# An attention-and-mixer kernel: in batches 4 and 6, v loads issued after the transposes of u, two features moved from VectorE to ScalarE, and k.v two slots later

## The chip, the cores and the metric

The kernel runs on one core of one Trainium2 chip. The metric is the time of one execution in microseconds (us) of device time. The kernel before was timed three times: 294.59, 293.90 and 294.26 us, median 294.26 us. The core has a matrix engine (TensorE, PE in the profile, with its weight loads as PEld), VectorE (DVE), ScalarE (ACT), GpSimd (POOL) and SyncE (SP), which here only issues DMAs. Each engine works through its own queue in the order in which the program gave it instructions, and waits on semaphores for what other engines or DMAs must have finished first.

## The reference

The inputs are q, k and v with 8 batches, 8 heads, 576 positions and 64 features per head, and the weights U, V, w1 and w2 of a mixer. Cut to what matters:

```python
# attention, per batch and head; c, s are cosine and sine weights of the position
q_p = concat(relu(q) * c, relu(q) * s)        # 128 features
k_p = concat(relu(k) * c, relu(k) * s)
kv  = k_p^T @ v            # 128 x 64
z   = sum over positions of k_p
x   = (q_p @ kv) / (q_p @ z + 1e-6)           # heads side by side: 576 x 512
# mixer, per batch
u   = x + (x^T @ U @ V)^T  # low rank mixing over positions
out = u + relu(u @ w1) @ w2                   # 512 -> 2048 -> 512
```

## The kernel before

**Tiles.** The 576 positions of a batch are four chunks of 128 rows (c = 0 to 3) and a tail of 64 (c = 4). Products take bf16 inputs and add in f32 PSUM banks.

**One list of slots.** The matrix work of the mixer is cut into 272 units, called slots, in one list (`lay_all`, L1057). Per batch there are the first units (u times w1, then relu: `g1_main` L670 and `g1_part` L596), and then the second units (the hidden layer times w2: `w_part` L829, 14 units, or `g2_part` for batch 0); behind odd batches there are units for the tails of the pair. `starts[b]` is the slot in which the first units of batch b begin: 0, 32, 70, 100, 138, 168, 202 and 232 for b = 0 to 7. Batches 3 and 5 are in `MIXED`: their first units use products of sums of blocks with seven multiplications in place of eight, whose right-hand sides (`tb`, four VectorE subtractions of blocks of the transposed u, `uT_form` L584) are formed in the four slots ahead of `starts[b]`. Their units come in the order `HALF = ("1", "s4", "6 2", "s5", "5 7", "s6", "3", "s7 4")`, where a digit is a part of the seven (`g1_part`) and "s4" to "s7" are plain units (`g1_main`). After a part or a plain unit, ScalarE (parts 1, 6, 5, 3 and all plain units) or VectorE (parts 2, 7, 4) takes the result out of PSUM.

**Work laid beside the slots.** The attention of batch b runs beside the mixer of the two batches before it. `attention_plan(b)` (L1083) names a slot for every step; after each slot's matrix unit, the steps planned for it are given to their engines, in the order of the batches. So a step's slot is its place in the queues, not a time. For b = 3 to 7 the steps are:

- `feature`: relu and weight of one chunk and one of cos and sin, first for q, then for k, 20 operations from slot F on. F is `starts[b-2]` + 16 for the batches 4 and 6, where G, which is `starts[b-1]`, lies 14 slots behind F. In each slot ScalarE takes one operation, and in some slots VectorE takes the next one as well.
- `v_prep`: casts of v to bf16 by GpSimd, from slot V0 on, which is `starts[b-2]` + 9.
- `qtr_dma`: transposes of q's features, as DMAs from SyncE's queue: tail, chunks 0 and 1, chunks 2 and 3.
- `kv_pair` (L344): 40 matrix products, k.v for all heads; they need every feature of k and every chunk of v. ScalarE takes the result out of PSUM (b > 3).
- `x_unit` for the five chunks (x from q's transposed features and k.v, with VectorE for the division), then `A_unit`, `u_va` and `u_add` (the low-rank part of u), then `utr_dma` (L518): the transposes of u, as DMAs from SyncE's queue, for the halves d = 0, 1 and d = 2, 3 and, in odd batches, for the tail rows.
- the loads of q, k and v of batch b + 1 (`loads` L983), at the three slots `at_load`. Each is three DMA issues on SyncE's queue (the tail L93, the odd rows L80, the even rows L87). The tiles for q, k and v as loaded are single, so each load waits until the features or casts of batch b have read the tile.

The slots that matter below are these. For b = 4: F = 86, G = 100, V0 = 79; the loads of q, k and v of batch 5 are at slots 94, 100 and 84, and k.v is at slot 101. At slots 84 and 86 lie the transposes of the u of batch 3 (both halves, and the tail at 86). For b = 6: F = 154, G = 168, V0 = 147; the loads of batch 7 are at 162, 168 and 152, k.v at 169; the transposes of the u of batch 5 at 151 and 153. The first `x_unit` is at G + 5 = 105 and 173.

Of the kernel before, what the change touches and what calls it, by code (L numbers as in the profile page):

```python
# [17 lines left out]
def kernel(  # L18
# [100 lines left out]
    V_, A_, G_ = nc.vector, nc.scalar, nc.gpsimd  # L119
# [125 lines left out]
    G3, T1, X1, OA, OB, O1 = ("g", 3), ("T", 1), ("X", 1), ("oA", 1), ("oB", 1), ("O", 1)  # L245
    X1S = ("x", 1)
# [528 lines left out]
    MIXED = {3: (0, 2), 5: (0, 2)}  # L775
# [207 lines left out]
    def loads(b):  # L983
        def thunk(dst, src):
            def go():
                load_tail(dst, src, b)
                load_main(dst, src, b)

            return go

        return thunk(qst, q), thunk(kst, k), thunk(vst, v)
# [91 lines left out]
    def attention_plan(b):  # L1083
        plan = []
        odd = b % 2 == 1

        def put(at, f, *a):
            plan.append((at, lambda: f(b, *a)))

        ops = [(f, c, i) for f in (q_prep, k_prep) for c in QORD for i in range(2)]  # L1090
        if b == 2:
            for n, (f, c, i) in enumerate(ops):
                if n < 8:
                    put((25, 26, 27, 28, 28, 29, 29, 30)[n], feature, f, c, i, A_)
                elif n < 10:
                    put(24 + n, feature, f, c, i, V_)
                else:
                    put(
                        (34, 34, 35, 36, 37, 38, 39, 39, 40, 41)[n - 10], feature, f, c, i,
                        A_ if n in (14, 17) else V_,  # L1100
                    )
            V0 = 33
            at_q, at_load = (32, 34, 36), (37, 42, 43)
            kv_at, x_at, a_at, u_at = 43, (44, 46, 48, 50, 52), 54, 55
            a_bank = O1
        else:
            F, G = starts[b - 2] + (20 if odd and b < B - 1 else 16), starts[b - 1]
            for s_ in range(G - F):
                for eng in (A_, V_)[: 1 + (s_ in ((0, 1, 2, 10, 11, 12) if b > 3 else (1, 2, 10, 11, 12)))]:
                    if ops:  # L1110
                        put(F + s_, feature, *ops.pop(0), eng)
            V0 = starts[b - 2] + 9 if b > 3 else F + 9
            at_q, at_load = (F + 5, F + 7, F + 7), (F + 8, F + 14, V0 + 5)
            if b == 3:
                at_q = (F + 6, F + 7, F + 8)
                at_load = (F + 11, F + 14, V0 + 5)
            X0 = G - 2 if odd else G
            x_at = [
                X0 + i for i in ((2, 4, 6, 9, 11) if b == 3 else (2, 4, 6, 8, 10) if odd else (3, 5, 7, 9, 11))
            ]  # L1120
            kv_at = X0
            if b in (4, 6):
                kv_at, x_at = G + 1, [G + i for i in (5, 8, 13, 16, 18)]
            elif b - 1 in MIXED:
                kv_at, x_at = G + 1, [G + i for i in ODDX]
            a_at = x_at[4] + (3 if b in (4, 6) else 2)
            u_at = a_at + 1
            a_bank = T1 if b == 3 else OB
        for n, c in enumerate(QORD):
            put(V0 + n, v_prep, 0, H, (c,), (G_,))  # L1130
        for at_, (c0, c1) in zip(at_q, ((4, 5), (0, 2), (2, 4))):
            put(at_, qtr_dma, c0, c1)
        put(kv_at, kv_pair, *X1)
        for n, c in enumerate(ORD):
            put(x_at[n], x_unit, c, *((O1, X1)[n % 2] if b < 4 else X1))
        put(a_at, A_unit, *a_bank, A_)
        put(u_at, u_va, (0, *X1), (2, *O1) if b < 4 else (2, OA, OB))
        put(u_at, u_add, 0)
        put(u_at + 2, u_add, 2)
        put(u_at + 2, utr_dma, 0, 2)  # L1140
        put(u_at + 4, utr_dma, 2, 4)
        if odd:
            put(*((u_at + 1, u_tail, *T1) if b < 4 else (u_at + 3, u_tail, *X1S)))
            put(u_at + 4, utr_dma, 4, 5)
        if b < B - 1:
            for at_, t in zip(at_load, loads(b + 1)):
                plan.append((at_, t))
        return plan
# [238 lines left out]
    for b in range(2, B):  # L1387
        for at, t in attention_plan(b):
            put(at, t)
# [34 lines left out]
```

## Time and profile before

| what | value |
|---|---|
| median of three runs | 294.26 us (293.90 to 294.59) |
| profiled execution, its own time | 294.26 us |
| span of its trace | 292.4 us |
| PE busy | 284.8 us, 97% of the span |
| DVE busy | 226.5 us, 77% |
| ACT busy | 159.8 us, 55% |
| POOL busy | 67.7 us, 23% |
| granted clock of TensorE | 1.00 throughout |
| moved by DMA | 53.32 MB, mean 182 GB/s |

The span runs from the first to the last instruction of the trace; the execution's own time is 1.86 us longer. A line of a timeline gives start, duration, engine, source line, operation, tiles and count, and in square brackets the idle time of the engine ahead of it with what ended that time; "L521" is line 521 of the kernel. The line of a helper stands for all its callers: L80, L87 and L93 are the loads of q, k and v, told apart by the tile (`qst`, `kst`, `vst`); L521 and L527 are the transposes of u and of its tail; L301 and L299 are features on VectorE and ScalarE; L350 is k.v. A stretch's table gives the busy time of each engine in it and the number of instructions. Durations of matrix products include the depth of the array: where products follow each other, the distance from start to start is the cost.

### The profile page before, as it was taken

The page shows a single profiled execution, that of the slowest core. Times are in us where ns is not written, and L with a number is a line of the kernel's source. Part 1 is how long each engine was busy: PE and PEld are TensorE (multiplying, and loading weights), DVE is VectorE, ACT ScalarE, POOL GpSimd, SP SyncE. Part 2 cuts the span into 40 slices and gives each one's busy share as a digit, 9 for nine tenths or more (in the row PEclk, how much of TensorE's full clock was granted, in tenths as well). Part 3 has the DMA queues.
Part 4 walks back from the last instruction along what each step waited for, and adds up shares of the span by engine and source line. Part 5 has one row for each costly group of instructions (what it writes and reads, how often), then busy time and mean ns, then how long its engine had stood idle before and what let it go on. Part 6 is the DMA issues. An engine that isn't in the chain of part 4 may idle for free.

```text
span 292.4 us, 7406 instructions
## 1 busy us (share of the span) xinstructions
PE 284.8 (97%) x3040; PEld 206.1 (70%) x3066; DVE 226.5 (77%) x452; ACT 159.8 (55%) x278; POOL 67.7 (23%) x104
## 2 busy tenths in 40 slices
PE   8999999999999999989999999999999999999995
PEld 6876455545987546866887555886888548899884
DVE  4989738887898768948897367868899686769974
ACT  2955651576593466846594365946792552067100
POOL 8330600050052303640023400450021102200210
PEclk9999999999999999999999999999999999999999
DMA  6999999998939899699957994999084304020023
GB/s 205 354 260 254 266 188 254 295 237 217 275 102 150 225 364 188 160 250 184 294 153 152 238 300 95 252 220 319 10 141 87 147 3 89 38 108 1 2 85 132
DMA packets 85445, 53.32 MB, mean 182 GB/s; under 512 B 53988, under 2 KB 83076, under 8 KB 85412
## 3 DMA queue, kind: packets, MB, share of 16 engines
q1 hardware_dynamic: 78996, 41.62, 60.3%
q0 software_dynamic: 6272, 11.17, 15.8%
q8 instruction: 24, 0.39, 0.6%
q14 instruction: 9, 0.07, 0.1%
q10 hardware_dynamic: 144, 0.07, 0.1%
HBM read 36.86 MB, written 9.44 MB: 158 GB/s over the span
## 4 chain that ended last, share of the span: by engine, by line
PE 78%; DMA 12%; DVE 4%; SPq 2%; issue 2%; ACT 0%; POOL 0%; DVEq 0%; POOLq 0%
PE w_ps L848 23%; PE g_ps L680 19%; PE gt_ps L701 5%; PE o_ps L741 5%; PE al_ps L629 5%; DMA kst<-in_k_dram 5%; PE be_ps L629 4%; PE w_ps L202 3%; DMA vst<-in_v_dram 3%; PE x_ps L425 3%; DMA w_bf<-in_moe_w_ch_dram 3%; PE kv_ps L350 3%; PE ot_ps L761 2%; PE ot_ps L949 2%; DMA uT<-u_bf 2%
## 5 line engine op out<-in xcount | busy, mean ns | idle before, releaser
L680 PE MATMUL g_ps<-uT,w_bf 128*128 128x512 bf16 x366 | 90.7, 379 | 0.8
L689 ACT ACTIVATE hid<-g_ps 128x512 bf16<-128x512 f32 x96 | 57.0, 597 | 47.1 <-PE g_ps L680 39.0
L680 PEld LDWEIGHTS <-w_bf 128*128 128x128 bf16 x384 | 34.8, 98 | 34.2 <-DMA w_bf<-in_moe_w_ch_dram 0.2
L860 POOL TENSOR_TENSOR o_sb<-w_sum,u_bf 128x512 f32<-128x512 f32 x14 | 22.0, 1588 | 119.3 <-DVE w_sum L860 119.3
L848 PEld LDWEIGHTS <-hid 128*128 128x128 bf16 x448 | 43.6, 98 | 5.6
L848 PEld LDWEIGHTS <-S 128*128 128x128 bf16 x336 | 32.4, 98 | 4.8 <-issue 0.5
L848 PE MATMUL w_ps<-w_bf,hid 128*128 128x256 bf16 x224 | 26.9, 273 | 0.0
L848 PE MATMUL w_ps<-T,hid 128*128 128x256 bf16 x224 | 26.9, 273 | 0.0
L848 PE MATMUL w_ps<-T,S 128*128 128x256 bf16 x224 | 26.3, 273 | 0.0
L646 DVE TENSOR_TENSOR hid<-pw,be_ps 128x512 bf16<-128x512 f32 x24 | 16.4, 685 | 10.9 <-PE be_ps L629 5.8
L114 ACT ACTIVATE pw<-al_ps 128x512 f32<-128x512 f32 x24 | 14.2, 596 | 18.2 <-PE al_ps L629 17.4
L492 DVE TENSOR_TENSOR u_bf<-x_bf,va_ps 128x1024 bf16<-128x1024 bf16 (+1 forms) x20 | 19.5, 1001 | 3.9 <-PE va_ps L481 3.9
L860 DVE TENSOR_TENSOR o_sb<-o_sb,w_ps 128x512 f32<-128x512 f32 x28 | 19.1, 682 | 3.7 <-PE w_ps L848 3.1
L435 DVE TENSOR_TENSOR x_bf<-x_ps,rec 128x512 bf16<-128x512 f32 x28 | 19.4, 692 | 1.0
L715 POOL DMA_DIRECT2D out_dram<-o_sb x12 | 7.6, 631 | 44.7 <-DVE o_sb L860 22.2
L299 ACT ACTIVATE k_p<-kst,sinw 128x512 bf16<-128x512 f32 x26 | 17.1, 712 | 0.0
L701 PE MATMUL gt_ps<-uT_tl,w_bf 128*128 128x128 bf16 x256 | 16.4, 219 | 0.0
L116 POOL CAST v_ext<-vst 128x512 bf16<-128x512 f32 x24 | 15.7, 696 | 2.9 <-DMA vst<-in_v_dram 2.7
L741 PE MATMUL o_ps<-w_bf,hid 128*128 128x512 bf16 x61 | 15.3, 379 | 0.6 <-DMA w_bf<-in_moe_w_ch_dram 0.4
L816 DVE TENSOR_TENSOR S<-hid,S 128x1024 bf16<-128x1024 bf16 x14 | 15.3, 1096 | 0.1
L701 PEld LDWEIGHTS <-w_bf 128*128 128x128 bf16 x256 | 15.0, 98 | 0.4
L299 ACT ACTIVATE q_p<-qst,cosw 128x512 bf16<-128x512 f32 x21 | 14.4, 712 | 0.1
(187 smaller groups left out, 469.2 us busy)
## 6 DMA issues: line engine op xcount, KB each, us to landing
qst<-in_q_dram SPq DMA_DIRECT2D x14, 512.0 KB, 6.0
kst<-in_k_dram SPq DMA_DIRECT2D x14, 512.0 KB, 8.4
vst<-in_v_dram SPq DMA_DIRECT2D x12, 512.0 KB, 8.3
out_dram<-o_sb POOLq DMA_DIRECT2D x12, 512.0 KB, 5.8
w_bf<-in_moe_w_ch_dram POOLq DMA_DIRECT2D x8, 512.0 KB, 10.3
out_dram<-o_sb SPq DMA_DIRECT2D x4, 512.0 KB, 3.1
qst<-in_q_dram SPq DMA_DIRECT2D x2, 640.0 KB
kst<-in_k_dram SPq DMA_DIRECT2D x2, 640.0 KB, 10.9
```

The lines of the kernel that those rows point to most:

```text
L116: eng.tensor_copy(out=o, in_=i)
L299: nc.scalar.activation(out=o, in_=i, func=AF.Relu, bias=0.0, scale=w)
L435: nc.vector.tensor_tensor(out=x_of(b, c, rows).rearrange("p (g i d) -> p g i d", g=2, d=D), in0=view[:, :, :, 0:D], in1=rec[rows].unsqueez ...
L492: nc.vector.tensor_tensor(out=u_bf[b][:, d0 : d0 + n], in0=x_bf[b].rearrange("p c (d n) -> p d c n", n=P)[:, d0 : d0 + n], in1=t.rearrange ...
L629: nc.tensor.matmul(out=res[:, k_, :], lhsT=lhs[:, d, k_, :], rhs=rhs[:, d, :], start=(opens and k_ == 0 and d == 0), stop=(k_ == 1 and d = ...
L646: V_.tensor_tensor(out=o, in0=x, in1=res, op=ALU.add)
L680: nc.tensor.matmul(out=g_ps.rearrange("p (c t) -> p c t", c=4), lhsT=w1_bf[:, d, j * P : j * P + P], rhs=uT[b][:, d, :, :], start=(d == 0) ...
L689: nc.scalar.activation(out=hid[b][:, j, :], in_=g_ps, func=AF.Relu, bias=0.0, scale=1.0)
L701: nc.tensor.matmul(out=g_ps[:, jj, :], lhsT=w1_bf[:, d, j * P : j * P + P], rhs=uT_tl[pr][:, d, :], start=(d == 0), stop=(d == 3),)
L741: nc.tensor.matmul(out=o, lhsT=hid[0][:, j, cc * P : cc * P + P], rhs=w2_bf[:, j, :], start=(j == 0), stop=(j == NJ - 1),)
L848: nc.tensor.matmul(out=res[:, g, :], lhsT=lhs[:, k_, g * P : g * P + P], rhs=rhs[:, k_, :], start=(opens and k_ == 0 and g == 0), stop=(k_ ...
L860: eng.tensor_tensor(out=o, in0=x, in1=y, op=ALU.add)
```

## The change

It touches `attention_plan` alone. For the batches 4 and 6:

- VectorE takes the second operation in the slots F, F+1, F+2 and F+8, in place of F, F+1, F+2, F+10, F+11 and F+12. The list of 20 features then reaches two slots further, to F+15, which is G+1; all features of q stay where they were.
- k.v moves from G+1 to G+3.
- The load of the next batch's k moves from F+14 to F+16, and that of the next batch's v from V0+5 to V0+8.

The lines with `d0` stand for all batches.

```diff
         else:
             F, G = starts[b - 2] + (20 if odd and b < B - 1 else 16), starts[b - 1]
-            for s_ in range(G - F):
-                for eng in (A_, V_)[: 1 + (s_ in ((0, 1, 2, 10, 11, 12) if b > 3 else (1, 2, 10, 11, 12)))]:
+            late = b in (4, 6)
+            both = (0, 1, 2, 8) if late else (0, 1, 2, 10, 11, 12) if b > 3 else (1, 2, 10, 11, 12)
+            for s_ in range(G - F + 2 * late):
+                for eng in (A_, V_)[: 1 + (s_ in both)]:
                     if ops:
                         put(F + s_, feature, *ops.pop(0), eng)
             V0 = starts[b - 2] + 9 if b > 3 else F + 9
-            at_q, at_load = (F + 5, F + 7, F + 7), (F + 8, F + 14, V0 + 5)
+            at_q, at_load = (F + 5, F + 7, F + 7), (F + 8, F + (16 if late else 14), V0 + (8 if late else 5))
...
-            if b in (4, 6):
-                kv_at, x_at = G + 1, [G + i for i in (5, 8, 13, 16, 18)]
+            if late:
+                kv_at, x_at = G + 3, [G + i for i in (5, 8, 13, 16, 18)]
...
-        put(u_at, u_add, 0)
-        put(u_at + 2, u_add, 2)
-        put(u_at + 2, utr_dma, 0, 2)
-        put(u_at + 4, utr_dma, 2, 4)
+        d0 = 2 if odd and b - 1 in MIXED else 0
+        put(u_at, u_add, d0)
+        put(u_at + 2, u_add, 2 - d0)
+        put(u_at + 2, utr_dma, d0, d0 + 2)
+        put(u_at + 4, utr_dma, 2 - d0, 4 - d0)
         if odd:
-            put(*((u_at + 1, u_tail, *T1) if b < 4 else (u_at + 3, u_tail, *X1S)))
-            put(u_at + 4, utr_dma, 4, 5)
+            put(*((u_at + 1, u_tail, *T1) if b < 4 else (u_at + 3 + d0, u_tail, *X1S)))
+            put(u_at + 4 + d0, utr_dma, 4, 5)
```

## The prediction

> **What bounds the kernel now.** I read the page first: its busy times and its chain of work that ended last.
>
> ```profile
> PE 284.8 (97%) x3040; PEld 206.1 (70%) x3066; DVE 226.5 (77%) x452; ACT 159.8 (55%) x278; POOL 67.7 (23%) x104
> PE 78%; DMA 12%; DVE 4%; SPq 2%; issue 2%; ACT 0%; POOL 0%; DVEq 0%; POOLq 0%
> ```
>
> PE is busy for 97% of the span, so a change of order can only win where PE stands still. Next I read the waits of PE from 100 us to the end, to see where it stands still behind another engine:
>
> ```profile
> PE kv_ps L350 <- DVE k_p L301: 0.9, 2, 0.5
> PE w_ps L848 <- DVE o_sb L860: 0.2, 1, 0.2
> ```
>
> Both waits of the first line lie in the one k.v (L350) of batch 4, and the change is about that place. The table of stretches around it, and PE's timeline inside it:
>
> ```profile
> 112.87:125.10 12.23, 12.23 (x113) 10.96 (x112) 10.55 (x16) 9.76 (x16) 7.41 (x8) 1.00 0.74 144
> 125.10:126.41 1.31, 1.26 (x10) 0.78 (x9) 0.38 (x2) 0.60 (x1) 0.14 (x1) 1.00 1.17 251
> 126.41:128.84 2.43, 1.52 (x41) 1.33 (x40) 2.10 (x6) 0.60 (x1) 0.36 (x1) 1.00 1.03 262
> ...
> 126.41 0.22 PE L350 MATMUL kv_ps<-v_ext,k_p 128*128 128x65 bf16 x2
> 127.00 0.19 PE L350 MATMUL kv_ps<-v_ext,k_p 128*128 128x65 bf16 x1 [0.37 <-DVE k_p L301]
> 127.73 0.19 PE L350 MATMUL kv_ps<-v_ext,k_p 128*128 128x65 bf16 x1 [0.54 <-DVE k_p L301]
> 128.84 0.60 PE L629 MATMUL al_ps<-tb,sa 128*128 128x256 bf16 x4
> ```
>
> The first number behind a stretch is its length, the second PE's busy time in it. The second units of batch 2 (112.87 to 125.10) run without a gap. k.v of batch 4 starts at 126.41 and the next unit at 128.84: 2.43 us. The same 40 products of batch 6 start at 193.60 and the next unit at 194.81: 1.21 us. So batch 4's k.v costs 2.43 - 1.21 = 1.22 us more than the work takes, 0.41% of the time. Batch 6 has no such gap; nor has any other stretch that the change touches.
>
> Why VectorE is late there, from its timeline and SyncE's:
>
> ```profile
> 123.63 0.69 DVE L860 TENSOR_TENSOR o_sb<-o_sb,w_ps 128x512 f32<-128x512 f32 x1
> 126.03 0.42 DVE L594 TENSOR_TENSOR tb<-uT,tb 128x512 bf16<-128x512 bf16 x1 [1.71 <-DMA uT<-u_bf]
> 126.37 0.48 DVE L301 TENSOR_SCALAR k_p<-kst,cosw 128x512 bf16<-128x512 f32 x1
> 127.10 0.48 DVE L301 TENSOR_SCALAR k_p<-kst,cosw 128x512 bf16<-128x512 f32 x1
> ...
> 111.18 1.25 SPq L521 DMA_TRANSPOSE uT<-u_bf  x1
> 112.48 0.62 SPq L93 DMA_DIRECT2D vst<-in_v_dram  x1
> 118.75 0.60 SPq L80 DMA_DIRECT2D vst<-in_v_dram  x1
> 119.45 0.60 SPq L87 DMA_DIRECT2D vst<-in_v_dram  x1
> 120.14 2.12 SPq L521 DMA_TRANSPOSE uT<-u_bf  x1
> 122.32 1.39 SPq L527 DMA_TRANSPOSE uT_tl<-u_tl  x1
> ```
>
> The second half of batch 3's u is ready when VectorE's addition ends at 113.06 (111.85 + 1.21), but its transpose is issued at 120.14. Ahead of it in SyncE's queue stands the load of the next v, which waits until GpSimd has cast the v of batch 4 (115.17 to 118.72). The transpose lands at about 125.93 in the chain. The second `tb` subtraction waits 1.71 us for it, and two k features that k.v needs stand behind that subtraction in VectorE's queue.
>
> **The load of v.** For batches 4 and 6 its three issues (L93, L80, L87) move behind two transposes, u's second half and its tail; they pass no other DMA, and q's transposes still come after them. In batch 4, SyncE is free at 112.43, so the second half is issued at about 113.1, 7 us earlier, the tail at about 115, and L80 still at 118.75, since GpSimd sets it. At the 4.9 us median that these transposes took to land, u is there by 120, and `tb` could start when the operation at 123.63 leaves VectorE, at 124.24. That ends the 1.71 us of idle time, by itself enough to bring both features ahead of k.v. What is late next is q's transposes, then the loads of q and k of batch 5: they stand behind L87 as before and move ahead by the 3.7 us from 120.14 to 123.81 that u's two transposes took. In batch 6 v's issues (178.80 to 180.80) move back to about 181 to 184. That v is cast from 194.57 on, and loads here took up to 11.6 us to land at the most; cost nothing.
>
> **The features.** Per batch VectorE loses operations 14, 16 and 18 of the list and gains 12: two fewer, 2 x 0.48 = 0.96 us. That is worth nothing in batch 6, where PE did not wait, and nothing more in batch 4 if the transposes are early. The operation added in slot F+8 is hidden there: the VectorE addition behind it (122.13 in batch 4) must be done before PE needs its bank at 125.10. ScalarE gets 2 x 0.61 us (its features follow each other 0.61 apart, 0.71 each). Seven k features end where seven ended before (123.43 and 190.64), and the last two fall into the slots G and G+1, behind the evacuations of those slots.
>
> **k.v two slots later.** The part "6 2" and the unit "s5" now run ahead of it; PE's order changes, not its work. Batch 4, on the times of before: part 6 at 126.41 (its `tb` ends at about 124.7), part 2 at 126.84, s5 at 127.28, k.v at 128.14, and its fourth product, the first that reads the last feature, at 128.24. ScalarE: evacuation of part 1 from 125.74, feature 18 from 126.24, evacuation of s4 from 126.85, feature 19 from 127.35 to 128.06; hand-over 0.12 (127.58 to the weight load at 127.70), so 128.18. In batch 6 the same sums give 195.38 ready against 195.43 needed. Without any overlap on ScalarE (0.60, 0.71, 0.60, 0.71 in a row, from 125.74 and 192.94) it is 128.48 and 195.68: 0.24 and 0.25 us late. So PE waits between 0 and 0.25 us per batch; I take 0, since the rows show the overlap (a feature starts 0.50 after an evacuation at 182.08, the next operation 0.61 after a feature). ScalarE's evacuation of k.v would end near 130.2, and the first x unit that reads it starts at 131.1 (132.31 less 1.22). GpSimd's casts of the next v wait for k.v and start some 0.5 us later; they are needed 30 us on. Queued behind the waiting evacuation on ScalarE is that of part 5; PE overwrites its bank only in part 3, two units later.
>
> **Loads of k, and the rest.** The k load moves two slots, past no other DMA: its queue neighbours are the q load and the v load of later slots. It waits for feature 19 (128.1 and 195.3), when SyncE is still at the q load or just past it (196 in batch 6 as before): nothing. `d0` is 0 for every batch: the keys of `MIXED` are 3 and 5, and the batch ahead of an odd one is even. Those lines change nothing.
>
> **Sum.** -1.22 (batch 4) + 0 (batch 6) + 0 (the last features, 0 to +0.50). The profiled execution took 294.26 us, 1.86 outside its span of 292.4, and equals the median of the runs: 294.26 - 1.22 = 293.04. After 128.84 VectorE waits again for PE or ScalarE (1.47, 0.76, 0.58 us of idle time up to 134.5), so what follows should shift as a whole.
>
> **A rule against it.** The Trainium skill, "Perfetto Trace Analysis", section "Optimizing Scalar/DVE Operations", says that an operation which either engine can do is faster on VectorE if that has a performance mode, and that moving it to ScalarE makes sense where VectorE is saturated. The rows agree on the price, 0.48 against 0.71 us; VectorE is not saturated at the end of these stages (0.40 and 0.62 us idle ahead of its additions near 190), which speaks against the move. By that rule the sum would lose up to the rival of the longer form below; by the row of ScalarE, idle for 2.31 and 2.30 us ahead of the evacuation of part 1, it loses nothing.
>
> **Rivals.**
> *Given back.* The time won is lost again between 145.6 and 159.3, where VectorE is busy 12.87 of 13.70 us and PE waits once for its addition (0.17 at 155.43). If something there does not move with PE, the time is 294.26, no change. Against it: VectorE's queue is fed by x units that PE runs earlier.
> *The longer form.* The four moved features cost 4 x (0.71 - 0.48) = 0.92 us on the path: 294.26 - 1.22 + 0.92 = 293.96, no change by measure. Against it stands ScalarE's idle time.
> *Slower: k.v waits for ScalarE.* If the two features given to ScalarE per batch come late by their whole 2 x 0.61 = 1.22 us, k.v waits so long in both batches: 294.26 - 1.22 + 2.44 = 295.48. For it: feature 19 has no slack to speak of (0.05 us). Against it: 0.25 is the most that these rows give. It turns to slower by over 0.59 us from a lateness of 0.91 us per batch.
> *The transposes do not land earlier*, because v of batch 4 is still in flight until 115.04. Then `tb` is ready at 126.45 and part 6 waits about 0.16, s5 about 0.11 for its bank, but k.v no longer waits: a gain of 0.95, 293.31. So either half of the change alone would take most of the gap; this is one with the forecast.
>
> **How the numbers follow.** Forecast with its variants (292.6 to 293.6): 0.74. Given back 0.10, longer form 0.06, slower 0.09, something else 0.01. About 0.2%, 0.59 us, is what a measurement can tell from no change here (the three runs spread 0.69). Faster 0.75, same 0.16, slower 0.09. The range reaches from 292.6, the sum less half the spread of the runs, to 294.3, which takes in the two rivals without change and leaves out the slower one. The forecast's own range is 292.6 to 293.6.
>
> **What would show it.** Right: u's second transpose issued near 113 and ahead of L93; no idle time ahead of the `tb` subtractions of batch 3; k.v of batch 4 in about 1.2 us from start to next unit, also in batch 6; later stages 1.2 us earlier. Wrong: idle time in k.v behind a ScalarE feature (L299), a new wait ahead of part 6 or s5, or a gap between 145 and 160 that grew.

## The result and the profile after

The changed kernel took 292.83 us (median of 11 runs, 292.37 to 294.02) against 293.90 us for the kernel before beside it (11 runs, 293.36 to 294.91): a ratio of 0.9962, 95% interval 0.9944 to 0.9979, 1.07 us faster. The profiled execution took 293.03 us and its trace spans 291.2 us, 1.2 us less than before.

From the page after, the busy times and the chain that ended last:

```profile
PE 283.6 (97%) x3040; PEld 204.7 (70%) x3066; DVE 224.1 (77%) x448; ACT 161.6 (56%) x282; POOL 68.4 (24%) x104
PE 89%; DMA 5%; DVE 2%; issue 1%; POOL 1%; SPq 0%; DVEq 0%
```

DVE has four instructions fewer and ACT four more: two features in each of the two batches. Before, the chain left PE at 98.56 us and came back to it only at 127.73, through the load of v, VectorE's queue and the transpose of u. From the chain before:

```profile
105.90 9.13 DMA vst<-in_v_dram
120.14 5.79 DMA uT<-u_bf
127.73 1.28 PE kv_ps L350 x37
```

Now it stays on PE from 94.46 to the end of k.v of batch 4 and beyond. (The shares alone don't show this: they also hold the start of the kernel, and a second profile of the changed kernel, e7, has DMA at 10%.) The waits of PE from 100 us to the end:

```profile
PE w_ps L848 <- DVE o_sb L860: 0.2, 1, 0.2
```

The two waits of k.v for VectorE's features are gone; the other one has stayed as it was. SyncE's timeline, and those of VectorE, ScalarE and PE around k.v of batch 4:

```profile
111.17 4.07 SPq L521 DMA_TRANSPOSE uT<-u_bf  x2
115.29 1.92 SPq L527 DMA_TRANSPOSE uT_tl<-u_tl  x1
117.27 0.62 SPq L93 DMA_DIRECT2D vst<-in_v_dram  x1
119.35 0.60 SPq L80 DMA_DIRECT2D vst<-in_v_dram  x1
120.76 1.25 SPq L399 DMA_TRANSPOSE q_tlT<-q_tl  x1
...
123.61 0.69 DVE L860 TENSOR_TENSOR o_sb<-o_sb,w_ps 128x512 f32<-128x512 f32 x1 [0.40 <-PE w_ps L848]
124.22 0.42 DVE L594 TENSOR_TENSOR tb<-uT,tb 128x512 bf16<-128x512 bf16 x1
124.56 0.42 DVE L594 TENSOR_TENSOR tb<-uT 128x512 bf16<-128x512 bf16 x1
126.22 0.71 ACT L299 ACTIVATE k_p<-kst,cosw 128x512 bf16<-128x512 f32 x1
126.39 0.60 PE L629 MATMUL al_ps<-tb,sa 128*128 128x256 bf16 x4
127.31 0.72 ACT L299 ACTIVATE k_p<-kst,sinw 128x512 bf16<-128x512 f32 x1
128.13 0.28 PE L350 MATMUL kv_ps<-v_ext,k_p 128*128 128x65 bf16 x4
129.34 0.60 PE L629 MATMUL al_ps<-tb,sa 128*128 128x256 bf16 x4
```

Both transposes of u's halves now leave one after the other, and the load of v comes behind them. VectorE goes from the addition at 123.61 straight into the `tb` subtraction at 124.22. The last k feature ends on ScalarE at 128.03, k.v starts at 128.13 and takes 1.21 us to the next unit. In batch 6 the same holds, with the feature ending at 194.01 and 1.20 us for k.v:

```profile
193.29 0.72 ACT L299 ACTIVATE k_p<-kst,sinw 128x512 bf16<-128x512 f32 x1
194.11 0.28 PE L350 MATMUL kv_ps<-v_ext,k_p 128*128 128x65 bf16 x4
195.31 0.60 PE L629 MATMUL al_ps<-tb,sa 128*128 128x256 bf16 x4
```

A measure inside the trace is sharper than the runs. The chain in order of time gives the start of k.v of batch 3 and the start of the last second units (batch 7). That stretch holds everything that the change touches, and not the beginning of the kernel: k.v of batch 3 starts anywhere between 93.86 and 96.39 us in the profiles below, though the kernels are alike up to there, and that alone is more than the effect. The stretch is 270.66 - 94.47 = 176.19 us before and 269.43 - 94.46 = 174.97 after, 1.22 us less.

| kernel (one profile each) | stretch, us | runs: ratio to before, interval |
|---|---|---|
| before | 176.19 | |
| before, again (e11) | 175.69 | |
| changed | 174.97 | 0.9962 (0.9944 to 0.9979) |
| changed, again (e7) | 174.96 | 0.9968 (0.9951 to 0.9985) |
| loads only (e1) | 174.98 | 0.9941 (0.9916 to 0.9966) |
| features, k.v and k's load (e8) | 175.44 | 0.9948 (0.9921 to 0.9976) |
| all but k.v's place (e3) | 178.21 | 1.0061 (1.0034 to 1.0088) |
| k.v's place only (e4; e9) | 175.26; 176.34 | 0.9990 (0.9963 to 1.0018) |
| batch 4 only (e5) | 174.96 | 0.9958 (0.9942 to 0.9975) |
| changed, u additions later (e6) | 174.88 | 0.9979 (0.9959 to 1.0000) |
| changed, one q feature moved (e10) | 174.62 | 0.9957 (0.9932 to 0.9982) |

### The profile page after: what moved, and what is told of

The parts are those of the page before. It is cut to its first block, busy times and chain, and to the rows that moved or that the text cites. A ratio compares the mean times of both kernels' runs of the same rounds, so it can differ in the third digit from the quotient of the medians.

```text
span 291.2 us, 7400 instructions
## 1 busy us (share of the span) xinstructions
PE 283.6 (97%) x3040; PEld 204.7 (70%) x3066; DVE 224.1 (77%) x448; ACT 161.6 (56%) x282; POOL 68.4 (24%) x104
## 4 chain that ended last, share of the span: by engine, by line
PE 89%; DMA 5%; DVE 2%; issue 1%; POOL 1%; SPq 0%; DVEq 0%
PE g_ps L680 29%; PE w_ps L848 28%; PE al_ps L629 5%; PE gt_ps L701 5%; PE o_ps L741 5%; PE be_ps L629 4%; PE x_ps L425 3%; DMA vst<-in_v_dram 3%; DMA w_bf<-in_moe_w_ch_dram 3%; PE kv_ps L350 2%; PE ot_ps L761 2%; PE ot_ps L949 2%; PE va_ps L481 1%; PE a_ps L451 1%; DVE u_bf L492 1%
## 5 line engine op out<-in xcount | busy, mean ns | idle before, releaser
L299 ACT ACTIVATE k_p<-kst,sinw 128x512 bf16<-128x512 f32 x26 | 17.7, 712 | 0.1
```

The costliest lines, as they stand in the source:

```text
L299: nc.scalar.activation(out=o, in_=i, func=AF.Relu, bias=0.0, scale=w)
```

## The experiments

Diffs are against the changed kernel unless they say otherwise. The ratios come from five rounds each beside the kernel before on the same chip. e1 to e4 shared one chip, e5 to e7 another, e8 to e11 a third, so ratios of different groups are not compared finely.

### e1: the loads alone

```diff
-            both = (0, 1, 2, 8) if late else (0, 1, 2, 10, 11, 12) if b > 3 else (1, 2, 10, 11, 12)
-            for s_ in range(G - F + 2 * late):
+            both = (0, 1, 2, 10, 11, 12) if b > 3 else (1, 2, 10, 11, 12)
+            for s_ in range(G - F):
...
-                kv_at, x_at = G + 3, [G + i for i in (5, 8, 13, 16, 18)]
+                kv_at, x_at = G + 1, [G + i for i in (5, 8, 13, 16, 18)]
```

> Only the loads of v and k move in batches 4 and 6; features and k.v stay as before. Theory (v's load holds back the transpose of u, that the tb subtraction, that two k features on VectorE, those k.v of batch 4): the transpose is issued near 113, tb starts at 124.2 without idle time, both features end before 126.4, k.v takes 1.2 us; 1.22 us faster than before (ratio 0.9959). Rival (what counts is that k.v comes two slots later and VectorE has less to do): k.v of batch 4 still takes 2.2 to 2.4 us and the time is that of before.

Measured: 292.90 against 294.50 us, ratio 0.9941 (0.9916 to 0.9966); the stretch is 174.98 us, 1.21 less than before and that of the whole change. SyncE, VectorE and PE:

```profile
110.57 4.01 SPq L521 DMA_TRANSPOSE uT<-u_bf  x2
...
123.62 0.42 DVE L594 TENSOR_TENSOR tb<-uT,tb 128x512 bf16<-128x512 bf16 x1
123.95 0.48 DVE L301 TENSOR_SCALAR k_p<-kst,cosw 128x512 bf16<-128x512 f32 x1
124.68 0.48 DVE L301 TENSOR_SCALAR k_p<-kst,cosw 128x512 bf16<-128x512 f32 x1
...
125.79 0.28 PE L350 MATMUL kv_ps<-v_ext,k_p 128*128 128x65 bf16 x4
127.00 0.60 PE L629 MATMUL al_ps<-tb,sa 128*128 128x256 bf16 x4
```

With the transposes early, both features leave VectorE by 125.16, ahead of k.v, which starts at 125.79 here and takes 1.21 us to the next unit. The theory's chain stands: load of v, transpose of u, `tb`, features, k.v. The loads alone give all of the gain; e1 moves the load of k as well, but that one stands behind the load of q in SyncE's queue before and after, and e8, which moves it without the load of v, leaves the transpose late. So it is the load of v, and the rival, that k.v's place and less work on VectorE make it, falls.

### e2 and e8: the features and k.v, without the loads

e2 left both loads where they were before:

```diff
-            at_q, at_load = (F + 5, F + 7, F + 7), (F + 8, F + (16 if late else 14), V0 + (8 if late else 5))
+            at_q, at_load = (F + 5, F + 7, F + 7), (F + 8, F + 14, V0 + 5)
```

> Only the features and k.v move; the loads stay as before. Theory: the transpose is still issued near 120 and lands near 126, VectorE still idles 1.7 us ahead of the second tb subtraction, but k.v needs nothing behind it; part 6 waits about 0.16 and the unit s5 about 0.11 us: 0.95 us faster than before (ratio 0.9968). Rival (the late transpose is what PE waits for, by whatever way): part 6, which now comes 1.2 us earlier, takes the wait over, and the time is that of before to 0.3 us faster.

Measured: 326.48 us, ratio 1.1080 (1.1026 to 1.1134). Neither theory had seen this. The load of the next k at slot G now stands in the program ahead of feature 19 at G + 1. So this kernel computes that feature (chunk 3, sine) of batches 4 and 6 from the k of the next batch, and it has to wait for that k to land; PE waits 28.0 us for it in the two k.v. So its time says nothing on the two theories. ScalarE's timeline:

```profile
127.76 0.60 ACT L689 ACTIVATE hid<-g_ps 128x512 bf16<-128x512 f32 x1 [0.58 <-ACT k_p L299]
145.84 0.72 ACT L299 ACTIVATE k_p<-kst,sinw 128x512 bf16<-128x512 f32 x1 [17.48 <-DMA kst<-in_k_dram]
```

The two slots of the k load were put at nothing, but without them the features cannot run on to G + 1. They belong to the features. e8 repeats the question with them:

```diff
-            at_q, at_load = (F + 5, F + 7, F + 7), (F + 8, F + (16 if late else 14), V0 + (8 if late else 5))
+            at_q, at_load = (F + 5, F + 7, F + 7), (F + 8, F + (16 if late else 14), V0 + 5)
```

> The features, k.v and the load of the next k move as in the change; only the load of the next v stays where it was. Measured within the trace, from the start of k.v of batch 3 to the start of the second units of batch 7: 176.19 us before, 174.97 changed. Theory: the transpose of u is late as before, VectorE waits for it ahead of the second tb subtraction, part 6 and s5 wait 0.1 to 0.2 us each at the most and k.v nothing: 175.0 to 175.3 us, and 0.9 to 1.2 us faster than before by the runs (ratio 0.996 to 0.997). Rival (the late transpose costs PE the same wherever it is met): 176 us or more, the time of before.

Measured: 293.38 against 294.38 us, ratio 0.9948 (0.9921 to 0.9976); the stretch is 175.44 us, a little above the 175.0 to 175.3 expected. VectorE and PE:

```profile
126.65 0.42 DVE L594 TENSOR_TENSOR tb<-uT,tb 128x512 bf16<-128x512 bf16 x1 [2.05 <-DMA uT<-u_bf]
...
125.39 0.60 PE L629 MATMUL al_ps<-uT,w_bf 128*128 128x256 bf16 x4
126.60 0.59 PE L680 MATMUL g_ps<-uT,w_bf 128*128 128x512 bf16 x2 [0.18 <-DMA uT<-u_bf]
127.13 0.61 PE L629 MATMUL al_ps<-tb,sa 128*128 128x256 bf16 x4
128.92 0.29 PE L350 MATMUL kv_ps<-v_ext,k_p 128*128 128x65 bf16 x4
```

The transpose is late by more than in the profile before (2.05 us of VectorE's time against 1.71), and still PE loses only 0.47 us (175.44 - 174.97), none of it in k.v. Nearly all of it lies ahead of part 6: that should follow 0.44 + 0.86 us behind 125.39, at 126.69, and starts at 127.13. The unit s4 itself reads the second half of the transposed u, and waits for it first. So the second half of the change works too: k.v no longer depends on the `tb` queue. It just has nothing left to do once the transposes are early. The rival of a wait that costs the same wherever it is met falls.

### e3: all but k.v's place

```diff
-                kv_at, x_at = G + 3, [G + i for i in (5, 8, 13, 16, 18)]
+                kv_at, x_at = G + 1, [G + i for i in (5, 8, 13, 16, 18)]
```

> The whole change, but k.v stays two slots ahead, at G + 1. Theory: the last k feature leaves ScalarE at 128.06 in batch 4 and about 195.3 on the clock of before in batch 6, 0.12 to the weight load, and the fourth product of k.v, due at 126.50 and 193.69, waits 1.68 and 1.69 us: 3.37 us slower than the changed kernel, 2.15 slower than before (ratio 1.007). Rival (the move of k.v is not needed once the transposes are early): the time of the changed kernel, 1.2 faster than before.

Measured: 296.32 against 294.50 us, ratio 1.0061 (1.0034 to 1.0088); the stretch is 178.21 us, 3.24 more than changed and 2.02 more than before (3.37 and 2.15 were expected). The waits of PE from 100 us on, and PE in k.v of batch 4:

```profile
PE kv_ps L350 <- ACT k_p L299: 2.9, 2, 1.4
...
128.70 0.20 PE L350 MATMUL kv_ps<-v_ext,k_p 128*128 128x65 bf16 x1 [1.44 <-ACT k_p L299]
```

That product was due at 127.09 (part 1 at 125.70, plus 0.44, 0.86 and 0.09), so it lost 1.61 us, twice: 3.2 us of the 3.24. The price of a late ScalarE feature is one for one in both batches, as the slower rival had it; the two slots of k.v are what keeps it at nothing.

### e4 and e9: k.v's place alone

Against the kernel before:

```diff
             if b in (4, 6):
-                kv_at, x_at = G + 1, [G + i for i in (5, 8, 13, 16, 18)]
+                kv_at, x_at = G + 3, [G + i for i in (5, 8, 13, 16, 18)]
```

> Only k.v moves two slots back; loads and features as before. Theory: the wait moves and stays. VectorE still reaches the second tb subtraction at 126.03 and the bank that s5 needs is freed by its addition behind the last feature, at 128.18: part 6 waits 0.16, s5 about 0.86 us, k.v nothing: 0.2 us faster than before, not to be told from no change (ratio 0.999). Rival (the two slots are enough): 1.2 us faster (0.996).

Measured: 294.40 against 294.50 us, ratio 0.9990 (0.9963 to 1.0018): no difference, as the theory said and against the rival's 0.996. But its profile fell on its fastest execution (292.79 us), in which VectorE waited only 0.29 us for the transpose, and showed no new wait. Its stretch, 175.26 us, is 0.29 above that of the changed kernel, but not by the moved work: from part 1 (124.81) to the unit behind k.v (129.06) PE takes 4.25 us, as in the changed kernel (125.09 to 129.34). The loss lies ahead of that, where products of the second units of batch 2 start at 119.31 and 121.32, 2.01 us apart for 1.75 of work. A transpose that came early can't tell the two theories apart, so the kernel was profiled once more:

> A second profile of the kernel in which only k.v moves: in the first one the transpose came early (VectorE waited 0.29 us for it), and that execution, 292.79 us, was the fastest of its kernel, whose median is 294.4. Theory: in a usual execution VectorE waits one to two us, part 6 waits little and s5 up to 0.9 us for its bank, so the stretch from k.v of batch 3 to the second units of batch 7 takes 175.5 to 176.0 us. Rival (the place of k.v was all): 175.0 us whenever the transpose comes.

Measured: one execution of 296.32 us; the stretch is 176.34 us, above the 175.5 to 176.0 expected. VectorE and PE:

```profile
128.38 0.42 DVE L594 TENSOR_TENSOR tb<-uT,tb 128x512 bf16<-128x512 bf16 x1 [2.15 <-DMA uT<-u_bf]
...
128.33 0.59 PE L680 MATMUL g_ps<-uT,w_bf 128*128 128x512 bf16 x2 [0.28 <-DMA uT<-u_bf]
130.58 1.02 PE L680 MATMUL g_ps<-uT,w_bf 128*128 128x512 bf16 x4 [0.67 <-DVE o_sb L860]
```

The wait has moved: s5 waits for the bank that VectorE's addition behind the last feature frees (0.83 us from where part 2 would let it start, 129.75, to 130.58; 0.86 had been worked out), and s4 and part 6 lose another 0.53. Moving k.v without taking features off VectorE exchanges one wait for another.

### e11: the kernel before once more

> A second profile of the kernel before, to see how far the delay of the transpose is the same from execution to execution. Theory: the load of v holds it back in every execution; VectorE waits 1 to 3 us ahead of the second tb subtraction and the stretch takes 175.8 to 177.5 us. Rival (the first profile was a rare one): no wait, 175.0 us.

Measured: one execution of 294.01 us; the stretch is 175.69 us, a little below the range expected, and VectorE waited 1.22 us:

```profile
125.79 0.42 DVE L594 TENSOR_TENSOR tb<-uT,tb 128x512 bf16<-128x512 bf16 x1 [1.22 <-DMA uT<-u_bf]
```

With the first profile there are two points: a wait of 1.71 us costs PE 176.19 - 174.97 = 1.22, a wait of 1.22 us costs 0.72. By these two, the first 0.5 us of VectorE's wait are free and the rest goes to PE one for one. So the gap that the change removes is not the same in every execution of the kernel before. The six profiles with v's load in its old place (before, e11, e2, e4, e8, e9) have VectorE waiting 0.29 to 2.59 us ahead of this subtraction. Part of that is when the transpose leaves, right behind v's load (25.67 us behind the start of k.v of batch 3 in the first profile, 25.05 in e4, 26.34 in e9), and part how long it is until VectorE goes on (5.89 us from its issue in the first profile, 5.38 in e11, which left as early).

### e5 and e7: batch 4 alone, and the change again

For e5, batch 6 keeps its old slots:

```diff
-            late = b in (4, 6)
+            late = b == 4
...
-            if late:
+            if b == 6:
+                kv_at, x_at = G + 1, [G + i for i in (5, 8, 13, 16, 18)]
+            elif late:
```

> The change for batch 4 alone; batch 6 as before. Theory: batch 6 had no gap, so its part is worth nothing: the time of the changed kernel, 1.22 us faster than before (ratio 0.9959), and k.v of batch 6 in 1.2 us. Rival (batch 6 gives some of the gain): less than that by what it gives.

e7 is the changed kernel beside it, on the same chip:

> The changed kernel beside the two others on the same chip: 1.22 us faster than before (ratio 0.9959).

Measured: 292.79 (e5) and 292.95 us (e7) against 294.10; ratios 0.9958 (0.9942 to 0.9975) and 0.9968 (0.9951 to 0.9985); stretches of 174.96 us both. Batch 6's part of the change is worth nothing.

### e6 and e10: the gap that is left

Between the second units of batch 3, PE loses 0.33 us (products start at 152.11 and 154.19, 2.08 us apart for 1.75 of work), before as after. e6 moves the two u additions that stand ahead of the awaited addition on VectorE:

```diff
-        put(u_at + 2, u_add, 2 - d0)
+        put(u_at + (4 if b == 4 else 2), u_add, 2 - d0)
```

> The changed kernel with one more step moved: in batch 4, u_add of the second half is two slots later, at u_at + 4, still ahead of its transpose. Theory: the gap of PE that is left between 145 and 160 (products of one part start at 152.11, the next part at 154.19: 2.08 us for 1.75 of work) is a wait for the addition that stands behind these two u additions (1.27 us) on VectorE; behind the addition they cost nothing: 0.33 us faster than the changed kernel, 1.55 faster than before (ratio 0.9947). Rival (VectorE has no room in this stage at all): the wait comes back at the next part, and the time is that of the changed kernel.

Measured: 293.36 us, ratio 0.9979 (0.9959 to 1.0000), not faster than e7; the stretch is 174.88 us, 0.08 less. The gap did close (products at 152.66 and 154.40). But u's second transpose leaves SyncE at 154.71 against 153.35 in e7, and q's transposes of batch 5 behind it at 156.04 against 154.69; 0.76 us of that is the later start of this execution (k.v of batch 3 at 95.01 against 94.25), the other 0.6 the moved additions. The second half of q's took 11.5 us to land, and an x unit waited for it. PE's x units in e6 and the waits from 160 to 176:

```profile
167.39 0.42 PE L425 MATMUL x_ps<-kv,q_pT 128*128 128x65 bf16 x8
169.64 0.43 PE L425 MATMUL x_ps<-kv,q_pT 128*128 128x65 bf16 x8
...
PEld L425 <- DMA q_pT<-q_p: 0.6, 1, 0.6
```

These units come 1.98 us apart elsewhere (165.41 to 167.39); here it is 2.25, so 0.27 us of the 0.33 are lost again. VectorE had room, as the theory said, and a wait came back, as the rival said, though not at the next part but one stage on. It took both the later issue and a longer way to land (11.5 us against 10.5 in e7); whether the second belongs to the moved additions, one profile doesn't show. e10 makes room on VectorE without a later transpose: one q feature of batch 5 goes to ScalarE, and the rest of that list moves on by one place.

```diff
-            both = (0, 1, 2, 8) if late else (0, 1, 2, 10, 11, 12) if b > 3 else (1, 2, 10, 11, 12)
+            both = (0, 1, 2, 8) if late else (0, 1, 10, 11, 12) if b == 5 else (0, 1, 2, 10, 11, 12) if b > 3 else (1, 2, 10, 11, 12)
```

> The changed kernel with one q feature less on VectorE in batch 5 (slots F, F+1, F+10, F+11, F+12 instead of also F+2; ScalarE takes it). Theory: VectorE's queue sets the addition that PE waits for at 154.19, by 0.33 us; 0.48 us less ahead of it ends the wait without a later transpose: the stretch takes 174.6 us against 174.97 of the changed kernel, 0.35 us faster by the runs. Rival (as when the u additions were moved: a wait comes back later): 174.9 to 175.0 us.

Measured: the stretch is 174.62 us, 0.35 less than changed, as worked out. The products start at 151.86 and 153.61, 1.75 us apart, and the list of PE's waits from 95 us to the end is empty. By the runs it took 293.16 against 294.38 us, ratio 0.9957 (0.9932 to 0.9982): faster than before. Whether it beats the changed kernel the runs don't tell; 0.35 us is within the intervals, and the two didn't run on the same chip.

## Why the prediction was right

Forecast were 293.04 us and a gain of 1.22; measured were 292.83 us and a gain of 1.07 by the medians of 11 runs, 1.22 by the stretch. The mechanism is as forecast. That the size agrees to 0.01 us is in part luck: the stretch of the changed kernel is compared with the very profile from which the gap was read, and against the second profile of the kernel before (e11) the gain is 0.72. The time came 0.21 us lower than forecast because the kernel before took 293.90 us beside it, 0.36 less than in the three runs that the forecast started from, and the gain was 0.15 smaller.

- **The load of v.** Right, and by e1 the whole of the gain. The second half was to leave at about 113.1 and the tail at about 115; the pair of halves took SyncE from 111.17 to 115.24 and the tail left at 115.29. The 4.9 us to landing was the time of a single transpose (the first half); in the changed kernel the second half left at 113.09 and took 5.5, still well ahead of 124. The `tb` subtraction was to start at 124.24 and started at 124.22. L80 was put at 118.75 and came at 119.35, since GpSimd ended its casts later here (119.32), and q's tail transpose moved ahead by 3.05 us in place of 3.7; nothing waited for either. In batch 6 the load of v took 2.9 to 5.8 us to land, well within the 11.6 allowed for.
- **The features.** Right: nothing in batch 6 (e5), nothing more in batch 4 (e1). The operation added in slot F+8 took 1.12 us, not 0.48, beside a GpSimd operation, and stayed hidden: the addition behind it was done at 122.88, PE needed its bank at 125.09.
- **k.v two slots later.** Right to 0.05 us: the last feature was worked out for 127.35 to 128.06 and ran from 127.31 to 128.03, k.v for 128.14 and started at 128.13. No wait in either batch, so 0 out of 0 to 0.25 was the value to take.
- **The loads of k.** "Nothing" was right for the time. What the step left out is that the move is a condition of the features' two slots (e2).
- **The rule of the Trainium skill**, "Perfetto Trace Analysis", section "Optimizing Scalar/DVE Operations", that the move to ScalarE makes sense where VectorE is saturated: VectorE was not, the price per operation was as in the rows before (0.71 against 0.48 us), and the path decided. In e3, with k.v two slots earlier, the slower place cost PE 1.61 us per batch; with k.v moved as well, nothing.
- **The rivals.** Given back: no; the gap near 154 is the same 0.33 us before and after, and the later stages start 1.23 us earlier (144.35 for 145.58, 269.43 for 270.66). The longer form: no. Slower by ScalarE: its mechanism is real (in e3 PE lost 1.61 us per batch where 1.68 had been worked out), but the condition was not met. Transposes not earlier: not the case, and as a variant (e8) it left 0.47 us of loss, not 0.27. The term at fault is the wait of part 6, put at 0.16: the unit s4 ahead of it reads the second half of u as well, and the transpose came later in that execution.
- **What the prediction did not see** is that the gap before differs between executions (0.72 and 1.22 us in two profiles). It took one profile's gap for the gap. The medians' 1.07 us lies between the two. Also, the lower end of the range is a slip of 0.1 us: 293.04 less half of 0.69 is 292.70, not 292.6; the result lies above either.

## What to carry to other kernels

Here the DMAs that SyncE issues stood in one line: a load that waited for GpSimd's casts until 118.75 us held back the transpose behind it until 120.14, though its data had been ready since 113.06, and the cost surfaced on PE, by way of VectorE's queue. So look for transfers that the matrix engine needs soon and put them ahead of those that wait for a buffer; that alone was worth the whole change. Read a gap from more than one profile before you price it. Before moving work to another place in a queue, count who reads what across the new order (e2), and look one stage on for the next thing in line (e6).

## What the runs showed of the hardware

- The time that a DMA transpose between two tiles on the chip took to land varied: u's halves 3.1 to 5.9 us in the profile before, with a median of 3.4, and the second half of q's 10.5 us in e7 and 11.5 in e6 at the same place. What makes the difference no run isolates. Margins worked out from a median are thin.
- A feature on VectorE took 1.12 us in place of 0.48 (start 121.17 in the changed kernel) while GpSimd ran its additions (119.29 to 122.00), and ended 0.29 us behind them. In e3, where it started at 122.87, behind the end of GpSimd's additions (122.59), it took 0.48. The Trainium skill, "SBUF — State Buffer", section "Who interferes with whom", says that a `tensor_scalar` on VectorE can run in a mode in which it and a GpSimd instruction shut each other out for a whole instruction. The rows agree in kind, though none shows that the feature ran in that mode; the feature ended sooner behind GpSimd than its own 0.48 us would have it, and GpSimd's ends are rough in the profile.
- The start of the kernel varies more than the effect: in the profiles k.v of batch 3 starts between 93.86 and 96.39 us, while the stretch behind it repeats to 0.02 us in four profiles in which the transposes are early and k.v waits for nothing (changed, e1, e5, e7: 174.96 to 174.98).
